# Rounding, loads and first splits around the end of a chunked-attention and two-layer feed-forward kernel's second up projection

## The chip, the cores and the metric

The kernel runs on one core of a Trainium2 chip. The metric is the device time of one execution, in microseconds (us). Engines are named as in the profile: PE is the matmul engine (TensorE) and PEld its weight load, DVE is VectorE, ACT is ScalarE, POOL is GpSimd, SP is SyncE, whose queue (SPq) issues every DMA of this kernel.

## What is computed

```python
attn_out = _attn_ref(**attn_kwargs)          # (4, 8, 768, 64), chunks of 32, softmax
x = attn_out.transpose(0, 2, 1, 3).reshape(B * S, H * D)   # 3072 x 512
h = x @ w_in;  r = maximum(h, 0);  g = s * (r * r) + b;  x = g @ w_out      # first layer
h = x @ w_in2; g = h - tanh(h);    return g @ w_out2                        # second layer
```

Both layers have 3072 tokens, a model width of 512 and a hidden width of 2048. All weights come as 64-bit floats and are read as pairs of 32-bit words.

## The kernel before, in words

Every fp32 product is made of three matmuls on rounded halves (`three`, lines 136 to 139): high by high, low by high, high by low. So each operand is first split: ACT rounds it to the high half, DVE subtracts to get the low half.

The program runs in stages: attention, the first layer's up projection (up 1), its down projection (down 1), then up 2 and down 2. The order on each engine is the order in which the code is written (`manual_schedule`, line 684); nothing reorders it. Each engine and the SP queue runs its own instructions in that order and waits where an operand or a buffer is not ready.

**Up 2** (lines 940 to 1000) goes over eight column blocks of the weights, `n` = 0 to 7. For each `n` there are three groups of 512-row token blocks. Groups 0 and 1 are plain products (`plain_column`, 12 matmuls each call, four calls per group; `plain_end` takes tanh on ACT at line 877 and subtracts on DVE at line 878). Group 2 (`quad`) computes its 2 by 2 blocks with seven products of Strassen's kind, P1 to P7 (`strassen`, six matmuls each). P1, P6, P5 and P3 add up in one PSUM bank, bank 0, and between them ACT copies the bank's state out (`copy`, line 900, into the tile `keep`): copy 1 after P1, copy 2 after P6, copy 3 after P5. P6 may not add to bank 0 before copy 1 has read it. P7 and P4 share bank 1, which `add` (line 903, DVE) reads before P4 adds to it. `curve` (lines 909, 910) makes the four tanh results, and `combine` (line 430) the sums that `end_out` stores to DRAM in the tiles `o2`, one per group, as `oa` (768 KB) and `ob` (1 MB).

Beside block `n`, the weights of block `n + 1` are made ready: ACT scales the raw words (line 144), DVE shifts, signs and fills them (lines 148, 152, 158), ACT rounds (`w2_high`, line 749), DVE subtracts (`w2_low`) and makes sums (`w2_sums`). In the last block (`n` = 7) the first weights of down 2 are prepared instead: quadrants 3 to 6 of `w_out` are fetched and converted (`load_quadrant`; "quadrant" here is one of its eight raw loads, 1 MB each, tile `raw`, line 364) and the weights of its first product are rounded (`high`, line 523, and `low`, line 528, tile `whl`).

**Down 2** (class `Down`, `run`, lines 564 to 580) walks over seven products (`ORDER`), three groups and two halves: 42 parts of 1 MB, read from `o2` (tile `part`, line 811). Each part is two entries. For entry `i`, `split` rounds 1024 columns on ACT (line 546) and subtracts on DVE (line 547) into a ring of three tiles, two entries ahead; `multiply(i)` does 12 matmuls. Part 0 holds the outputs of `n` = 0 to 3 of group 0; part 1 those of `n` = 4 to 7 of group 0; parts 2, 3 and 4, 5 the same of groups 1 and 2. The table `WEIGHTS` says behind which entry of a product the next product's weights are summed, rounded and subtracted; it serves down 1 and down 2. `between2` converts the last quadrants of `w_out` behind given entries.

In the text below, "multiply 7" is `multiply(7)` of down 2, "split 10" its `split(10)`; high and low half are the ACT and the DVE instruction of a split.

Of the kernel before, what the change touches and what calls it, by code (L numbers as in the profile page):

```python
# [48 lines left out]
"""  # L49

WEIGHTS = {
    (0, 1): [("sums", 1, 0)], (0, 2): [("high", 1, 0)], (0, 4): [("low", 1, 0)],
    (0, 5): [("sums", 1, 1)], (0, 6): [("high", 1, 1)], (0, 8): [("low", 1, 1)],
    (2, 0): [("sums", 3, 0)], (2, 1): [("high", 3, 0)], (2, 2): [("low", 3, 0)],
    (2, 4): [("sums", 3, 1)], (2, 5): [("high", 3, 1)], (2, 6): [("low", 3, 1)],
    (2, 8): [("sums", 4, 0)], (2, 9): [("sums", 4, 1)],
# [15 lines left out]
def tile_chunk_attention_two_ffn(  # L72
# [365 lines left out]
    class Down:  # L438


        def __init__(self, src, zmap, smap, whl, stream, ring, load, view, pick, bias, final, turn):
            self.src, self.zmap, self.smap, self.whl, self.stream, self.ring = src, zmap, smap, whl, stream, ring
            self.load, self.view, self.pick, self.bias, self.final = load, view, pick, bias, final
            self.z, self.zt, self.st, self.w, self.part, self.xs, self.ps = {}, {}, {}, {}, {}, {}, {}
            self.loaded, self.turn = 0, turn
            self.parts = [(p, g, h) for p in range(7) for g in range(NG) for h in range(2)]
            self.entries = [(p, g, h, e) for p, g, h in self.parts for e in range(2)]
            self.quads = list(zmap)
# [115 lines left out]
        def run(self, between):  # L564
            deep = len(self.stream)
            self.load_to(deep - 1)
            n = len(self.entries)
            for i in range(2):
                if i not in self.xs:
                    self.split(i)  # L570
            for i in range(n):
                if i + 2 < n:
                    self.split(i + 2)
                    if i % 2:
                        self.load_to(i // 2 + 1 + deep)
                self.multiply(i)
                p, k = divmod(i, 4 * NG)
                for step, q, half in WEIGHTS.get((p, k), ()):
                    getattr(self, step)(q, half)
                between(p, k)  # L580
# [117 lines left out]
    for j in range(2, NBLK):  # L698
        last = j == NBLK - 1
# [41 lines left out]
    def w2_signed(n):  # L741
        signed(w2_z[n], w2[n])

    def w2_filled(n):
        filled(w2_z[n], w2.pop(n))
# [120 lines left out]
    def plain_column(n, g, i, col):  # L866
        ps = bank2(2 + i)
        wh, wl = wi[2, n]
        for c in range(KD):
            xh, xl = x2_of(c, 1 - col, g)  # L870
            three(ps[:, col, 0:NB], wh[:, i, c, :], wl[:, i, c, :], xh, xl, c == 0, c == KD - 1)
# [11 lines left out]
    def strassen(name):  # L883
        acc = bank(chain[name])
        wh, wl = w2_hl[name]
        xh, xl = x2[operand[name], NG - 1]
        new_ = name in ("P1", "P7", "P2")
        for c in range(2):
            three(acc, wh[:, c], wl[:, c], xh[:, c], xl[:, c], c == 0 and new_, c == 1, not new_)

    def quad(n):
        g = NG - 1
        begin_out(n, g)
        oa = outs[n, g][0]
        keep = new(C_SNAP[0], 2 * NB, F32, "keep")
        snap = {1: keep[:, 0:NB], 2: keep[:, NB:2 * NB], 3: new(C_SNAP[1], NB, F32, "keep3")}
        rs = {}

        def copy(q):
            nc.scalar.activation(out=snap[q], in_=bank(0), func=AF.Copy)  # L900

        def add(o, q, k):
            nc.vector.tensor_tensor(out=oa[:, o], in0=snap[q], in1=bank(k), op=ALU.add)

        def curve(o, src):
            if o // 2 not in rs:
                rs[o // 2] = new(C_R[o // 2], 2 * NB, F32, "r2").rearrange("p (m t) -> p m t", m=2)
            r = rs[o // 2][:, o % 2]
            nc.scalar.activation(out=r, in_=src, func=AF.Tanh)
            nc.vector.tensor_tensor(out=oa[:, o], in0=src, in1=r, op=ALU.subtract)  # L910

        strassen("P1")
        copy(1)
        strassen("P7")
        strassen("P6")
        copy(2)
        yield
        strassen("P5")
        copy(3)
        strassen("P2")  # L920
        add(2, 3, 1)
        strassen("P3")
        add(1, 1, 2)
        strassen("P4")
        yield
        curve(0, bank(0))
        curve(1, oa[:, 1])
        curve(2, oa[:, 2])
        add(3, 2, 1)
        curve(3, oa[:, 3])  # L930
        yield
        end_out(n, g)
        yield
# [3 lines left out]
    def fetch(k, place=0):  # L937
        quads[k] = down2.load_quadrant(D_RAW[place])

    group = None  # L940
    for n in range(8):
        last = n == 7
        before = group
        begin_out(n, 0)
        for col in range(2):
            plain_column(n, 0, 0, col)
        if before is not None:
            next(before)
        if n in (2, 4, 6):
            quads[n // 2 - 1]()  # L950
        if not last:
            w2_load(n + 1)
        else:
            fetch(3, 0)
            fetch(4, 1)
        plain_end(n, 0, 0)
        if before is not None:
            next(before)
        if n == 0:
            t_split("T3")  # L960
            t_split("T2")
        w2_split(n)
        for col in range(2):
            plain_column(n, 0, 1, col)
        plain_end(n, 0, 1)
        end_out(n, 0)
        if n == 0:
            t_split("T1")
            t_split("T4")
        begin_out(n, 1)  # L970
        for col in range(2):
            plain_column(n, 1, 0, col)
        if last:
            quads[3]()
            down2.sums(0, 0)
            down2.high(0, 0)
            down2.low(0, 0)
            fetch(5, 0)
        else:
            w2_steps[0](n + 1)  # L980
        plain_end(n, 1, 0)
        if last:
            quads[4]()
            fetch(6, 1)
            down2.sums(0, 1)
            down2.high(0, 1)
            down2.low(0, 1)
            down2.load_to(0)
        else:
            for step in w2_steps[1:]:  # L990
                step(n + 1)
            if n in (1, 3, 5):
                fetch(n // 2)
        plain_column(n, 1, 1, 0)
        group = quad(n)
        next(group)
        plain_column(n, 1, 1, 1)
        plain_end(n, 1, 1)
        next(group)
        end_out(n, 1)  # L1000
    down2.load_to(1)
    down2.split(0)
    down2.split(1)
    next(group)

    def between2(p, k):
        if p == 0 and k == 0:
            next(group)
        if p == 0 and k == 3:
            quads[5]()  # L1010
            fetch(7, 0)
        if p == 1 and k == 6:
            quads[6]()
        if p == 1 and k == 9:
            quads[7]()
# [73 lines left out]
```

## Time and profile before

| | |
|---|---|
| median of three runs | 1091.02 us (1090.01 to 1091.71) |
| the profiled execution's own time | 1092.42 us |
| its span, first to last instruction | 1090.6 us |
| PE busy | 1055.8 us, 97% of the span |
| DVE busy | 813.3 us, 75% |
| ACT busy | 510.4 us, 47% |
| mean granted clock of PE | 0.993 |
| DMA | 242.15 MB, mean 222 GB/s |

Times in the trace are counted from the first instruction. Attention and up 1 end at 354 us, down 1 at 584, up 2 at 846; down 2 takes the rest, its last matmul starting at 1085.3. A matmul of 512 columns is shown with a duration near 0.39 us, but matmuls are pipelined: what one costs is the distance from its start to the next start. Idle time in square brackets stands before the instruction and names what ended it.

### The profile page before, as it was taken

How to read it: one execution, taken by the hardware profiler on the slowest of the kernel's cores; microseconds unless marked ns; L12 is line 12 of the kernel's file. 1: busy time of each engine (PE TensorE's matmuls, PEld its weight loads, DVE VectorE, ACT ScalarE, POOL GpSimd, SP SyncE). 2: the span in 40 equal slices, each digit the busy share in tenths (PEclk: the TensorE clock that was granted, in tenths of full speed). 3: DMA queues.
4: the chain of work that ended last, by engine and by line, in shares of the span. 5: the costliest groups of instructions: out<-in, count | busy, mean ns of one | idle time of the engine just before them, and what ended most of it. 6: DMA issues, size and time to landing. Idle time of an engine off the chain costs nothing.

```text
span 1090.6 us, 15131 instructions
## 1 busy us (share of the span) xinstructions
PE 1055.8 (97%) x6024; PEld 867.5 (80%) x6024; DVE 813.3 (75%) x969; ACT 510.4 (47%) x914; POOL 2.7 (0%) x24
## 2 busy tenths in 40 slices
PE   5999999999999999999999999999999799999998
PEld 4878888888888888888888777787778578888886
DVE  7997667777768866777787677787788778776654
ACT  7673655555433554455544333333334545444432
POOL 1000000000000000000000000000000000000000
PEclk8999999999999999999999999999999999999999
DMA  9864778775459756555541455655468975566751
GB/s 316 262 248 179 247 254 301 250 252 205 174 217 328 285 193 193 193 193 193 193 154 61 151 218 199 266 207 221 174 227 329 364 286 192 194 223 240 245 199 58
DMA packets 71686, 242.15 MB, mean 222 GB/s; under 512 B 5312, under 2 KB 5312, under 8 KB 61376
## 3 DMA queue, kind: packets, MB, share of 16 engines
q1 hardware_dynamic: 71616, 241.19, 61.8%
q8 instruction: 47, 0.77, 0.3%
q14 instruction: 23, 0.19, 0.1%
HBM read 146.80 MB, written 94.37 MB: 221 GB/s over the span
## 4 chain that ended last, share of the span: by engine, by line
PE 80%; DVE 9%; ACT 4%; DMA 4%; issue 2%; SPq 0%; ACTq 0%; DVEq 0%
PE pb L137 26%; PE pb L139 25%; PE pb L138 25%; PE pb L314 2%; PE pb L292 1%; DVE z L158 1%; PE pb L252 1%; DVE ob L430 1%; DVE z L152 1%; ACT sm L276 1%; DMA raw<-in_wo_dram 1%; DMA o<-oa 1%; DMA part<-o 1%; ACT w L749 1%; ACT r L877 1%
## 5 line engine op out<-in xcount | busy, mean ns | idle before, releaser
L137 PE MATMUL pb<-ringhringl,whl 128*128 128x512 f32 x672 | 262.4, 390 | 4.9 <-ACT ringhringl L546 4.9
L139 PE MATMUL pb<-ringhringl,whl 128*128 128x512 f32 x672 | 263.0, 391 | 3.0 <-DVE ringhringl L547 2.8
L138 PE MATMUL pb<-ringhringl,whl 128*128 128x512 f32 x672 | 262.0, 390 | 0.0
L547 DVE TENSOR_TENSOR ringhringl<-part,ringhringl 128x1024 fp32r<-128x1024 f32 x120 | 146.4, 1223 | 78.5 <-ACT ringhringl L546 78.5
L546 ACT ACTIVATE ringhringl<-part 128x1024 fp32r<-128x1024 f32 x120 | 126.3, 1059 | 150.2 <-PE pb L139 133.2
L137 PE MATMUL pb<-xh,w 128*128 128x512 f32 (+1 forms) x392 | 153.6, 392 | 0.6 <-DVE oa L415 0.3
L139 PEld LDWEIGHTS pb<-ringhringl,whl 128*128 128x128 f32 x672 | 126.4, 188 | 33.4 <-DVE ringhringl L547 6.6
L139 PE MATMUL pb<-xl,w 128*128 128x512 f32 (+1 forms) x392 | 151.2, 386 | 0.8 <-DVE xl L336 0.8
L138 PE MATMUL pb<-xh,w 128*128 128x512 f32 (+1 forms) x392 | 151.1, 386 | 0.5 <-DVE w L385 0.5
L137 PEld LDWEIGHTS pb<-ringhringl,whl 128*128 128x128 f32 x672 | 126.4, 188 | 31.5 <-ACT ringhringl L546 5.7
L138 PEld LDWEIGHTS pb<-ringhringl,whl 128*128 128x128 f32 x672 | 126.5, 188 | 26.4
L405 ACT ACTIVATE r<-pb 128x512 f32<-128x512 f32 x96 | 55.7, 591 | 100.7 <-PE pb L139 88.5
L415 DVE SCALAR_TENSOR_TENSOR oa<-pb,s_c,r 128x512 f32<-128x512 f32 x96 | 70.0, 745 | 29.2 <-ACT r L405 29.2
L137 PEld LDWEIGHTS pb<-xh,w 128*128 128x128 f32 x392 | 73.6, 188 | 17.7 <-DVE oa L415 1.8
L276 ACT ACTIVATE sm<-sm,nmx 128x96 f32<-128x96 f32 x192 | 69.1, 363 | 37.8 <-DVE nmx L270 37.8
L139 PEld LDWEIGHTS pb<-xl,w 128*128 128x128 f32 x392 | 73.6, 188 | 15.9 <-DVE xl L336 1.0
L138 PEld LDWEIGHTS pb<-xh,w 128*128 128x128 f32 x392 | 73.7, 188 | 14.9 <-DVE w L385 0.9
L542 DVE SCALAR_TENSOR_TENSOR ringhringl<-part,b_c,ringhringl 128x1024 fp32r<-128x1024 f32 x48 | 61.3, 1283 | 25.2 <-ACT ringhringl L541 24.8
L139 PE MATMUL pb<-x2hx2l,w 128*128 128x512 f32 x192 | 74.7, 389 | 0.0
L138 PE MATMUL pb<-x2hx2l,w 128*128 128x512 f32 x192 | 74.7, 389 | 0.0
L137 PE MATMUL pb<-x2hx2l,w 128*128 128x512 f32 x192 | 74.7, 389 | 0.0
L541 ACT ACTIVATE ringhringl<-part,b_c 128x1024 fp32r<-128x1024 f32 x48 | 54.9, 1147 | 36.3 <-PE pb L139 33.5
(131 smaller groups left out, 1394.8 us busy)
## 6 DMA issues: line engine op xcount, KB each, us to landing
o<-ob SPq DMA_DIRECT2D x48, 1024.0 KB, 4.9
part<-o SPq DMA_DIRECT2D x84, 512.0 KB, 4.6
part<-o SPq DMA_DIRECT2D x42, 1024.0 KB, 5.0
o<-oa SPq DMA_DIRECT2D x48, 768.0 KB, 3.9
raw<-in_wi_dram SPq DMA_DIRECT2D x16, 1024.0 KB, 7.2
raw<-in_wo_dram SPq DMA_DIRECT2D x16, 1024.0 KB, 7.2
qk<-in_qk_dram SPq DMA_DIRECT2D x24, 640.0 KB, 7.9
v<-in_vw_dram SPq DMA_DIRECT2D x24, 384.0 KB, 8.1
```

The lines of the kernel that those rows point to most:

```text
L137: nc.tensor.matmul(acc, lhsT=whi, rhs=xhi, start=first, stop=False, skip_group_check=more)
L138: nc.tensor.matmul(acc, lhsT=wlo, rhs=xhi, start=False, stop=False, skip_group_check=more)
L139: nc.tensor.matmul(acc, lhsT=whi, rhs=xlo, start=False, stop=last, skip_group_check=more)
L152: nc.vector.scalar_tensor_tensor(out=zi, in0=hi32, scalar=-(1 << 31), in1=zi, op0=ALU.bitwise_and, op1=ALU.bitwise_or)
L276: nc.scalar.activation(out=sm[:, h, :], in_=sm[:, h, :], func=AF.Exp, bias=nmx[:, h:h + 1], scale=1.0, accum_out=sums[:, h:h + 1],)
L314: nc.tensor.matmul(value_bank(u)[64 * g:64 * g + 64, c0:c0 + QE], lhsT=tv[0:KE, e, 2 * r + g, :], rhs=pt[0:KE, 4 * g + r, QE * e:QE * (e + ...
L405: nc.scalar.activation(out=r, in_=up_ps[j, t], func=AF.Relu)
L415: nc.vector.scalar_tensor_tensor(out=oab[j, q][0][:, 2 * i:2 * i + 2, k, :], in0=ps2, scalar=s_c[:, 0:1], in1=r2, op0=ALU.mult, op1=ALU.mult,)
L541: nc.scalar.activation(out=xh, in_=src, func=AF.Identity, bias=self.bias)
L542: nc.vector.scalar_tensor_tensor(out=xl, in0=src, scalar=self.bias, in1=xh.bitcast(F32), op0=ALU.add, op1=ALU.subtract)
L546: nc.scalar.activation(out=xh, in_=src, func=AF.Copy)
L547: nc.vector.tensor_tensor(out=xl, in0=src, in1=xh.bitcast(F32), op=ALU.subtract)
```

## The change

Four places of the written order change; no instruction is added or removed.

1. `WEIGHTS`, product 0: the two sums, the rounding and the low half of the next product's weights move from behind entries 1, 2, 4 (first half) and 5, 6, 8 (second half) to behind entries 4, 5, 6 and 8, 9, 10. Down 1 and down 2 both read the table.
2. `Down` gets `ahead`, 1 for down 1 (as before) and -1 for down 2: down 2's loads of parts are written two parts later.
3. In up 2, `quad` stops once more, behind copy 1. For `n` below 7, `w2_high`, `w2_low` and `w2_sums` are written there, between copy 1 and P7, and no longer ahead of P1.
4. In the last block, part 0 of down 2 is loaded in front of the two `w_out` loads; the rounding of the first product's weights moves behind quadrant 4's conversion; splits 0 and 1 are written behind copy 2; parts 1 and 2 are loaded ahead of group 1's stores; group 2's curves move behind multiply 0 and its stores behind multiply 1; quadrant 5's conversion and the fetch of quadrant 7 move from behind multiply 3 to behind multiply 7.

```diff
 WEIGHTS = {
-    (0, 1): [("sums", 1, 0)], (0, 2): [("high", 1, 0)], (0, 4): [("low", 1, 0)],
-    (0, 5): [("sums", 1, 1)], (0, 6): [("high", 1, 1)], (0, 8): [("low", 1, 1)],
+    (0, 4): [("sums", 1, 0)], (0, 5): [("high", 1, 0)], (0, 6): [("low", 1, 0)],
+    (0, 8): [("sums", 1, 1)], (0, 9): [("high", 1, 1)], (0, 10): [("low", 1, 1)],
...
-            self.loaded, self.turn = 0, turn
+            self.loaded, self.turn, self.ahead = 0, turn, 1 - 2 * turn
...
                     if i % 2:
-                        self.load_to(i // 2 + 1 + deep)
+                        self.load_to(i // 2 + deep + self.ahead)
...
         strassen("P1")
         copy(1)
+        yield
         strassen("P7")
...
         if last:
+            down2.load_to(0)
             quads[3]()
-            down2.sums(0, 0)
-            down2.high(0, 0)
-            down2.low(0, 0)
             fetch(5, 0)
...
         if last:
             quads[4]()
             fetch(6, 1)
-            down2.sums(0, 1)
-            down2.high(0, 1)
-            down2.low(0, 1)
-            down2.load_to(0)
+            for half in range(2):
+                down2.sums(0, half)
+                down2.high(0, half)
+                down2.low(0, half)
         else:
-            for step in w2_steps[1:]:
-                step(n + 1)
-            if n in (1, 3, 5):
-                fetch(n // 2)
+            w2_signed(n + 1)
+            w2_filled(n + 1)
         plain_column(n, 1, 1, 0)
         group = quad(n)
         next(group)
+        if not last:
+            w2_high(n + 1)
+            w2_low(n + 1)
+            w2_sums(n + 1)
+            if n in (1, 3, 5):
+                fetch(n // 2)
+        next(group)
+        if last:
+            down2.split(0)
+            down2.split(1)
         plain_column(n, 1, 1, 1)
         plain_end(n, 1, 1)
         next(group)
+        if last:
+            down2.load_to(2)
         end_out(n, 1)
-    down2.load_to(1)
-    down2.split(0)
-    down2.split(1)
-    next(group)

     def between2(p, k):
-        if p == 0 and k == 0:
+        if p == 0 and k in (0, 1):
             next(group)
-        if p == 0 and k == 3:
+        if p == 0 and k == 7:
             quads[5]()
             fetch(7, 0)
```

How the instructions stand in the built programs, first on ACT in up 2, block `n` = 0 (blocks 1 to 6 read the same). `w<-z` is the rounding of the next block's weights, `keep<-pb` are copies 1 and 2, `r<-pb` the tanh of a plain group; - is before, + is the change:

```order
 L877 ACTIVATE r_5172<-pb 128x1024
-L749 ACTIVATE w<-z 128x1024
-L900 ACTIVATE keep<-pb 128x512 x2
+L900 ACTIVATE keep<-pb 128x512
+L749 ACTIVATE w<-z 128x1024
+L900 ACTIVATE keep<-pb 128x512
 L877 ACTIVATE r_5232<-pb 128x1024
```

The rounding has moved from ahead of copy 1 to between copy 1 and copy 2.

Second, the SP queue in the last block of up 2. `o_0_79`, `o_1_80` and `o_2_81` are the tiles `o2` of groups 0, 1 and 2; rows with `part<-` are down 2's loads, rows with `<-oa` and `<-ob` are stores of up 2:

```order
 L864 DMA o_0_79<-ob 128x2048
+L811 DMA part<-o_0_79 128x4x512
 L364 DMA raw<-in_wo_dram 128x2048 x2
 L811 DMA part<-o_0_79 128x4x512
-L863 DMA o_1_80<-oa 128x1536
-L864 DMA o_1_80<-ob 128x2048
-L811 DMA part<-o_0_79 128x4x512
-L811 DMA part<-o_1_80 128x4x512 x2
+L811 DMA part<-o_1_80 128x4x512
+L863 DMA o_1_80<-oa 128x1536
+L864 DMA o_1_80<-ob 128x2048
+L811 DMA part<-o_1_80 128x4x512
```

Part 0 stands ahead of the two raw loads, and parts 1 and 2 stand behind them and ahead of group 1's stores.

Third, the passage from up 2 to down 2. On ACT before, from copies 1 and 2 of block 7 on (`r` from `oa` and the second `r` from `pb` are the curves of group 2, `ringhringl<-part` the high halves of splits):

```order
L900 ACTIVATE keep<-pb 128x512 x2
L877 ACTIVATE r_6735<-pb 128x1024
L900 ACTIVATE keep_6702<-pb 128x512
L546 ACTIVATE ringhringl<-part 128x1024 x2
L909 ACTIVATE r_6779<-pb 128x512
L909 ACTIVATE r_6779<-oa 128x512
L909 ACTIVATE r_6784<-oa 128x512 x2
```

and in the changed program:

```order
L900 ACTIVATE keep<-pb 128x512 x2
L546 ACTIVATE ringhringl<-part 128x1024 x2
L877 ACTIVATE r_6741<-pb 128x1024
L900 ACTIVATE keep_6702<-pb 128x512
L546 ACTIVATE ringhringl<-part 128x1024
L909 ACTIVATE r_6800<-pb 128x512
L909 ACTIVATE r_6800<-oa 128x512
L909 ACTIVATE r_6805<-oa 128x512 x2
```

The high halves of splits 0 and 1 stand behind copy 2, ahead of the last plain tanh and copy 3; that of split 2 stands ahead of the curves. On DVE in down 2's first product, before, from the sums of the next weights' first half (`s<-zq`) on; `zq` rows are quadrant 5's conversion, `whl` the low half of weights, `ringhringl` the low halves of splits:

```order
L501 TENSOR_TENSOR s_6836<-zq 128x1024
L501 TENSOR_TENSOR s_6838<-s_6836,zq 128x1024
L547 TENSOR_TENSOR ringhringl<-part,ringhringl 128x1024 x2
L148 TENSOR_SCALAR zq<-zq 128x1024
L152 SCALAR_TENSOR_TENSOR zq<-raw,zq 128x1024
L158 SCALAR_TENSOR_TENSOR zq<-raw,zq 128x1024
L547 TENSOR_TENSOR ringhringl<-part,ringhringl 128x1024
L528 TENSOR_TENSOR whl<-s_6838,whl 128x1024
```

and in the changed program:

```order
L501 TENSOR_TENSOR s_6881<-zq 128x1024
L501 TENSOR_TENSOR s_6883<-s_6881,zq 128x1024
L547 TENSOR_TENSOR ringhringl<-part,ringhringl 128x1024 x2
L528 TENSOR_TENSOR whl<-s_6883,whl 128x1024
L547 TENSOR_TENSOR ringhringl<-part,ringhringl 128x1024
L148 TENSOR_SCALAR zq<-zq 128x1024
L152 SCALAR_TENSOR_TENSOR zq<-raw,zq 128x1024
L158 SCALAR_TENSOR_TENSOR zq<-raw,zq 128x1024
L547 TENSOR_TENSOR ringhringl<-part,ringhringl 128x1024
L501 TENSOR_TENSOR s_6961<-zq 128x1024
L501 TENSOR_TENSOR s_6963<-s_6961,zq 128x1024
L547 TENSOR_TENSOR ringhringl<-part,ringhringl 128x1024 x2
```

Before, the sums stood between splits 3 and 4 and the conversion between splits 5 and 6; now the sums stand between splits 6 and 7, the conversion between splits 9 and 10, and the second half's sums between splits 10 and 11.

## Rows read from the trace of the kernel before

**Rows 1.** The page, part 1: busy time, share of the span, instructions of each engine.

```profile
PE 1055.8 (97%) x6024; PEld 867.5 (80%) x6024; DVE 813.3 (75%) x969; ACT 510.4 (47%) x914; POOL 2.7 (0%) x24
```

**Rows 2.** PE's waits: us in total, times, longest us.

```profile
PE pb L137 <- ACT keep L900: 7.8, 7, 2.0
...
PE pb L137 <- ACT ringhringl L546: 4.9, 2, 2.7
...
PE pb L139 <- DVE ringhringl L547: 2.8, 5, 1.5
```

**Rows 3.** Timeline of PE in up 2: start us, duration us, instruction [idle before].

```profile
608.25 0.51 PE L137 MATMUL pb<-t,shl 128*128 128x512 f32 x1 [2.00 <-ACT keep L900]
...
611.97 0.43 PE L137 MATMUL pb<-x2h,w 128*128 128x512 f32 x1
...
641.06 0.39 PE L139 MATMUL pb<-t,shl 128*128 128x512 f32 x1
642.35 0.50 PE L137 MATMUL pb<-t,shl 128*128 128x512 f32 x1 [0.91 <-ACT keep L900]
```

**Rows 4.** Timeline of DVE in block 1 of up 2.

```profile
639.50 1.23 DVE L158 SCALAR_TENSOR_TENSOR z<-raw,z 128x1024 int32<-128x1024 int32 x1
```

**Rows 5.** Timeline of ACT in block 1 of up 2.

```profile
640.76 1.06 ACT L749 ACTIVATE w<-z 128x1024 fp32r<-128x1024 f32 x1 [3.68 <-DVE z L158]
641.72 0.58 ACT L900 ACTIVATE keep<-pb 128x512 f32<-128x512 f32 x1
```

**Rows 6.** Stretches: us, busy by engine (instructions), granted PE clock, DMA share, GB/s.

```profile
608.25:611.90 3.65, 3.65 (x9) 2.93 (x10) 2.41 (x5) 0.60 (x1) 0.00 (x0) 0.55 0.00 0
...
857.70:861.10 3.40, 3.25 (x7) 2.14 (x8) 3.37 (x5) 1.88 (x2) 0.00 (x0) 0.51 1.05 385
```

**Rows 7.** Timeline of PE from block 7 of up 2 into down 2.

```profile
831.10 0.39 PE L137 MATMUL pb<-x2hx2l,w 128*128 128x512 f32 x1
...
844.70 0.39 PE L137 MATMUL pb<-t,w 128*128 128x512 f32 x1
...
845.83 0.39 PE L139 MATMUL pb<-t,w 128*128 128x512 f32 x1
...
879.10 0.50 PE L139 MATMUL pb<-ringhringl,whl 128*128 128x512 f32 x1
879.43 0.39 PE L137 MATMUL pb<-ringhringl,whl 128*128 128x512 f32 x1
```

**Rows 8.** Timeline of the SP queue around the end of up 2.

```profile
830.70 0.32 SPq L864 DMA_DIRECT2D o<-ob  x1
...
839.64 0.43 SPq L811 DMA_DIRECT2D part<-o  x1
...
847.29 5.63 SPq L811 DMA_DIRECT2D part<-o  x4
```

**Rows 9.** DMA issues, us to landing: at 830.7, 839.6 and 849.2 us, and after 900.

```profile
o<-ob SPq DMA_DIRECT2D x1, 1024.0 KB, 5.0
...
part<-o SPq DMA_DIRECT2D x1, 1024.0 KB, 7.6
...
part<-o SPq DMA_DIRECT2D x1, 1024.0 KB, 12.8
...
part<-o SPq DMA_DIRECT2D x29, 1024.0 KB, 4.9
```

**Rows 10.** Timeline of ACT: copy 2 of block 7, and the first sum of down 2.

```profile
838.10 0.60 ACT L900 ACTIVATE keep<-pb 128x512 f32<-128x512 f32 x1 [2.12 <-PE pb L139]
...
866.84 1.01 ACT L829 ACTIVATE sumX<-pb 128x1024 f32<-128x1024 f32 x1
```

**Rows 11.** Timeline of DVE: block 7's last weights, split 6, the second half's sums.

```profile
839.10 1.22 DVE L528 TENSOR_TENSOR whl<-zq,whl 128x1024 fp32r<-128x1024 f32 x1
...
872.02 1.22 DVE L547 TENSOR_TENSOR ringhringl<-part,ringhringl 128x1024 fp32r<-128x1024 f32 x1
...
875.43 1.22 DVE L501 TENSOR_TENSOR s<-zq 128x1024 f32<-128x1024 f32 x1
```

## The prediction

> **What bounds the kernel now.** I read the page's busy times first. PE is busy for 97% of the span [rows 1] and no other engine comes near, so whatever ends earlier must end PE's waits or make its matmuls start closer together. The second view is the list of PE's waits [rows 2]. Leaving out the first 30 us, which the change doesn't touch, three lines hold nearly all of it: seven waits for copy 1 (7.8 us, "ACT keep"), two for the high half of a split (4.9) and five for a low half (2.8). The third view is PE's timeline around them. It gives what an undisturbed matmul costs: 65 steps lie between 831.10 and 845.83 [rows 7], so 0.2266 us each. Against that, a wait costs more than its idle time. In block 1 of up 2 the step into P6 is 641.06 to 642.35 [rows 3], 1.29 us, that is 1.06 over an undisturbed one where the row says 0.91 idle: the idle time plus about 0.16. The step behind a wait is long too: 879.10 to 879.43 [rows 7], 0.33, which is 0.10 over. So a wait costs its idle time plus 0.27.
>
> **Up 2 (part 3 of the change).** Why does P6 wait? In block 1 filling the next weights starts on DVE at 639.50 and lasts to 640.73 [rows 4]; the rounding on ACT waits for that, starts at 640.76, and copy 1 follows at 641.72 [rows 5]. P1 itself had been done long before: its last matmul starts six steps ahead of the one at 641.06 [rows 3], at 639.70, and with the 0.39 that the rows show it ends at 640.09. So copy 1 is held by its neighbour in the queue, not by its data. In the new order it takes 640.1 to 640.7, P6 can start at 641.29 on its undisturbed step, and the rounding still starts at 640.76, since that is when its own data come. The wait is gone with 0.6 us to spare. What is late next would be copy 2: it stands behind the rounding now, which ends at 641.8, before P6 has ended (about 642.8); and P5, which needs copy 2, is 12 matmuls (2.7 us) further on. I cost that at nothing.
>
> The sum for seven blocks: 7.8 us idle [rows 2] plus 7 times 0.27 is 9.7. In block 0 a second cost hangs on the wait. From 608.25 to 611.97 nine steps take 3.72 us [rows 3] instead of 2.04, because the granted clock stands at 0.55 there [rows 6], close to the lower of its two levels (1.2 of 2.4 GHz). The dip follows straight on a wait of 2.00 us [rows 3], the longest of the seven [rows 2]. With the wait gone I take the dip as gone: 1.68, of which 0.10 is counted already. **Up 2 gains 11.3 us.**
>
> **The passage into down 2 (parts 2 and 4).** What is lost there today can be had in one line. The matmul at 879.10 is the third of multiply 8, number 98 counted from multiply 0's first. Undisturbed that first one stands one step behind 845.83, at 846.06, and number 98 at 868.27. It starts at 879.10 [rows 7], and one more 0.10 follows: 10.9 us, dip at 857.70 included [rows 6]. Behind it PE runs on without stops to its last matmul, so this loss reaches the end undiminished.
>
> The reason stands in the SP queue [rows 8]: part 0 is issued at 839.64, behind a raw load, and parts 1 to 4 only from 847.29, behind group 1's stores, which wait for DVE. Part 0 lands 7.6 us after its issue, at 847.2 [rows 9], when PE has stood since 846.2. In the new order part 0 follows the store of 830.70, so it is issued at 831.1. That store lands after 5.0 us, at 835.7. One megabyte behind another at 385 GB/s [rows 6] takes 2.7 us, so part 0 lands at 838.4, or at worst some way behind. Copy 2 of block 7 ends at 838.70 [rows 10], and split 0 is next on ACT: it just fits. Splits 0 and 1 then keep ACT for 1.9 us, until the last plain tanh can begin. On DVE the last low half of weights ends near 840.3 [rows 11]; two low halves, the plain subtraction (each of them 1.14 behind the one before) and the add that frees bank 1 bring it to 844.3, while P4 wants the bank at 844.70 [rows 7]: it fits by 0.4. Multiply 0 starts on its undisturbed step.
>
> Three losses stay.
> - **Parts 1 and 2.** Part 1 is issued behind the second raw load, which waits for quadrant 4's conversion: about 838.5, with part 0 and two raw loads, 8 us of transfer, in front. It should land near 846.5, then split 2, the four curves, split 3 and group 2's four sums queue on ACT and DVE in front of split 4. Bounds: nothing, where they all fit; 2.7, today's longest single wait [rows 2], which is this same part's, issued 8.8 later [rows 8]. I take 1.2, nearer to nothing, because most of the lateness goes.
> - **Quadrant 5's conversion** now stands in front of split 10's low half. Today the same chain, from the sum at 866.84 [rows 10] to the end of split 6 at 873.24 [rows 11], takes 6.4 us. In the new place the sum starts 0.43 behind multiply 7's last start, and multiply 10's third matmul, the first to need that low half, comes 27 steps (6.12) behind it. 0.43 + 6.4 + 0.08 to pass it on, less 6.12, is 0.8, and 0.1 for the step behind it: 0.9.
> - **The second half's sums** follow at once. Two of 1.2 each [rows 11] and a low half make 3.5; multiply 11's third matmul comes 2.8 later than multiply 10's. 0.7, with the step 0.8.
>
> Together 2.9 of the 10.9 stay; **the passage gains 8.0 us.** A price from a page: the Trainium skill, DMA: Bandwidth & Descriptors, section Anatomy of one DMA, fits the time of a DMA (of another issuing path) as 2.0 us plus its bytes at 436 GB/s. My estimate from it is 4.4 us for 1 MB; by it part 1 lands at 842.9, the first of the three losses vanishes and the time comes out 1.2 lower than below. The rows agree for a lone part (4.9) and not for parts in company (7.6 and 12.8) [rows 9].
>
> **What I cost at nothing.** `WEIGHTS` in down 1: PE's list has no wait for the biased splits of its first product [rows 2], so there is nothing to gain; the sums bring two 1.2 us instructions between splits there as here, but no conversion stands beside them. Bound: 1.5, as the third loss for both halves. Loads two parts later: a part's issue waits for its buffer, so the written place decides only whether a store stands in front. Counting the entries between a store's end and the split that needs the part, six entries or 16.3 us less 1.3 for the store's own instruction are left, 15.0, against 4.9 to land [rows 9]. Raw loads 2.7 later: their conversions stand behind multiply 7 and later, over 20 us on.
>
> **The sum.** 11.3 + 8.0 = 19.3. The profiled execution took 1092.42, so 1073.1 of that kind; it lies 1.4 above the median of the runs, 1091.02, so the median should come to **1071.7 us**.
>
> **Rivals.**
> - **Part 0 lands late and ACT and DVE hand it on.** Split 0 stands in front of the last tanh and copy 3 on ACT, and in front of the add that frees bank 1 on DVE. From 0.4 us of lateness on, P3 and P4 stop for the rest. For it: its margin is the smallest of all, and loads in company were slow [rows 9]. Against it: two transfers at most are in front. Half of the worst, 2.6 late, costs 2.2 and 0.4 for two steps, and about 0.7 more on split 4: 1075.0. At today's worst landing, 12.8, it is 5.2 late, P4 stops for over 2 us and a dip like those of rows 6 follows, 1.7: some 4.8 + 0.4 + 1.7 less the 1.2 of part 1, which then waits anyway: 1077.4. The Trainium skill, same page, section Queues, rings and completion order, says that each DMA engine takes descriptors in ring order; by that the raw load issued later can't push part 0 back, the sum stands and this rival has less for it, and the rows, where landings follow the issues, agree.
> - **Parts land early.** If part 1 takes 4.9 us like a lone one [rows 9], it is there at 843.4 and the first loss vanishes: 1070.5. Against it: 7.6 in company today [rows 9]. The page's fit, above, speaks for it.
> - **The wait moves on to copy 2.** If the rounding were as late as P6's end, P5 would stop in each block. It would give half of up 2's gain back: 1077.3. Against it: 2.7 us and more of cover in block 1.
> - **Slower: the loads of down 2 come too late.** With stores ahead of them on SP, each of the 24 parts of the last four products has 15.0 us from issue to use. If they land later than that, PE waits in each of them. The change loses only past 16 us to landing, where 24 times 0.9 is 21.6: 1093.3. Against it: 4.9 after 900 us, 12.8 at worst in the crowd [rows 9].
> - **The reordering in up 2 does nothing**: P6 is held by something other than copy 1. Then only the passage counts: 1083.0. The rows name copy 1 in all seven, so this is thin.
>
> **How the numbers follow.** The forecast 0.74, with its own range 1070 to 1074; late part 0 0.15; early parts 0.04; copy 2 0.03; up 2 unmoved 0.02; late loads of down 2 0.02, half of that so little late that it just uses up the gain. The lower end takes all three losses as nothing but 0.6: 1069.5. The upper end reaches into the first two rivals: 1077.0. A difference of 0.2% (2.2 us) is about what a measurement of this kernel can tell from none: faster 0.98, same 0.01, slower 0.01.
>
> **What would show it.** Right: "ACT keep" is gone from PE's waits and the clock stays full near 608; P6 follows P7 by 0.23 us; part 0 is issued near 831 and multiply 0 starts one step behind P4; waits of about 0.7 at multiplies 10 and 11. Wrong: PE waiting for L900 at P5, or for L903 at P4; a dip behind 846; waits for "part" after 900.

## The result and the profile after

The changed kernel takes 1072.95 us (median of 4 runs, 1072.36 to 1074.0) against 1090.95 in the same comparison: a ratio of 0.9837, with a 95% interval of 0.9819 to 0.9854. That is 18.0 us less, where 19.3 were forecast; 1071.7 was the forecast, 1069.5 to 1077.0 its range. The profiled execution took 1072.36 us with a span of 1070.6. One execution of experiment 2, a slow one of 2139.27 us, is left out of its median below.

The page, part 1, and the first three lines of the list of PE's waits (us in total, times, longest) of the changed kernel, beside [rows 1, 2]:

```profile
PE 1050.6 (98%) x6024; PEld 867.5 (81%) x6024; DVE 812.9 (76%) x969; ACT 511.5 (48%) x914; POOL 2.7 (0%) x24
```

```profile
PE pb L252 <- DMA qk<-in_qk_dram: 5.6, 3, 4.7
PE pb L292 <- DVE sm L286: 3.0, 3, 2.6
PE pb L139 <- DVE ringhringl L547: 2.1, 4, 0.7
```

The waits for copy 1 ("ACT keep") and for high halves ("ACT ringhringl") are gone from the list. What leads it now belongs to attention's start. Low halves still cost 2.1 us idle, 0.3 of it in down 1 as before.

Up 2, block 1, in the changed kernel. First ACT, where copy 1 now stands ahead of the rounding, then DVE, which ends the filling of the rounding's data:

```profile
635.84 0.60 ACT L900 ACTIVATE keep<-pb 128x512 f32<-128x512 f32 x1 [3.05 <-PE pb L139]
636.47 1.06 ACT L749 ACTIVATE w<-z 128x1024 fp32r<-128x1024 f32 x1
638.56 0.60 ACT L900 ACTIVATE keep<-pb 128x512 f32<-128x512 f32 x1 [1.03 <-PE pb L139]
```

```profile
635.21 1.22 DVE L158 SCALAR_TENSOR_TENSOR z<-raw,z 128x1024 int32<-128x1024 int32 x1
```

Copy 1 waits for P1 alone now and is done 0.03 us before the rounding starts, which starts 0.04 after its data at 636.43, as it did before [rows 4, 5]. Copy 2 waits for P6, with ACT idle for 1.03 before it. That cover is not the same in every block: ACT is idle for 0.39 in block 6, and in block 0 copy 2 follows the rounding with no idle time between. PE is not held in either. PE takes the step from P7 into P6 without a stop, 636.77 to 637.00:

```profile
636.77 0.39 PE L139 MATMUL pb<-t,shl 128*128 128x512 f32 x1
637.00 0.39 PE L137 MATMUL pb<-t,shl 128*128 128x512 f32 x1
```

The passage, in the changed kernel: the SP queue, then the landing time of the part issued at 819.25, then ACT, then PE from P4 into multiply 0 and at its three stops in down 2.

```profile
818.84 0.32 SPq L864 DMA_DIRECT2D o<-ob  x1
819.25 0.39 SPq L811 DMA_DIRECT2D part<-o  x1
822.01 4.58 SPq L364 DMA_DIRECT2D raw<-in_wo_dram  x2
826.68 0.94 SPq L811 DMA_DIRECT2D part<-o  x2
```

```profile
part<-o SPq DMA_DIRECT2D x1, 1024.0 KB, 8.1
```

```profile
826.24 0.60 ACT L900 ACTIVATE keep<-pb 128x512 f32<-128x512 f32 x1 [2.12 <-PE pb L139]
827.33 2.01 ACT L546 ACTIVATE ringhringl<-part 128x1024 fp32r<-128x1024 f32 x2 [0.49 <-DMA part<-o]
```

```profile
833.97 0.39 PE L139 MATMUL pb<-t,w 128*128 128x512 f32 x1
834.20 0.39 PE L137 MATMUL pb<-ringhringl,whl 128*128 128x512 f32 x1
...
846.38 0.50 PE L139 MATMUL pb<-ringhringl,whl 128*128 128x512 f32 x1 [0.66 <-DVE ringhringl L547]
...
863.61 0.50 PE L139 MATMUL pb<-ringhringl,whl 128*128 128x512 f32 x1 [0.61 <-DVE ringhringl L547]
...
867.14 0.50 PE L139 MATMUL pb<-ringhringl,whl 128*128 128x512 f32 x1 [0.52 <-DVE ringhringl L547]
```

Part 0 lands 8.1 us after its issue, at 827.3, and split 0 starts 0.49 later than ACT could have begun it. That is inside the margin, by little: the add that frees bank 1 ends 0.3 us before P4 starts. Multiply 0 starts one step behind P4, where there were 2.55 us before, from 845.83 [rows 7] to this row of the kernel before:

```profile
848.38 0.50 PE L137 MATMUL pb<-ringhringl,whl 128*128 128x512 f32 x1 [2.16 <-ACT ringhringl L546]
```

The three stops left are at multiplies 4, 10 and 11. With the step of 0.34 behind each they cost 0.93, 0.89 and 0.79 (a step into the third matmul of 1.04, 1.00 and 0.90, each less 0.2266, and 0.11): 2.6 of the 10.9 us.

Where the 20.0 us between the two spans came from, by the starts of PE's matmuls: up 2, from its first matmul to its last, takes 250.0 us instead of 261.5 (11.5 gained), from there to the last matmul of all 231.2 instead of 239.4 (8.2), and down 1 began 0.4 earlier, at 353.76 instead of 354.14.

### The profile page after: what moved, and what is told of

The parts are those of the page before. It is cut to its first block, busy times and chain, and to the rows that moved or that the text cites. A ratio compares the mean times of both kernels' runs of the same rounds, so it can differ in the third digit from the quotient of the medians.

```text
span 1070.6 us, 15128 instructions
## 1 busy us (share of the span) xinstructions
PE 1050.6 (98%) x6024; PEld 867.5 (81%) x6024; DVE 812.9 (76%) x969; ACT 511.5 (48%) x914; POOL 2.7 (0%) x24
## 4 chain that ended last, share of the span: by engine, by line
PE 87%; DVE 7%; ACT 2%; DMA 2%; issue 1%; SPq 0%; ACTq 0%; DVEq 0%
PE pb L137 28%; PE pb L139 27%; PE pb L138 27%; PE pb L314 2%; PE pb L292 2%; PE pb L252 1%; ACT sm L276 1%; DVE ob L430 1%; DMA part<-o 1%; DVE ringhringl L547 1%; DVE oa L415 1%; DMA raw<-in_wi_dram 1%; DVE z L158 1%; DVE w L385 1%; DVE z L152 0%
## 5 line engine op out<-in xcount | busy, mean ns | idle before, releaser
L137 PE MATMUL pb<-ringhringl,whl 128*128 128x512 f32 x672 | 261.5, 389 | 0.0
L138 PE MATMUL pb<-ringhringl,whl 128*128 128x512 f32 x672 | 261.5, 389 | 0.0
L137 PEld LDWEIGHTS pb<-xh,w 128*128 128x128 f32 x392 | 73.6, 188 | 17.6 <-DVE oa L415 1.6
```

The costliest lines, as they stand in the source:

```text
L137: nc.tensor.matmul(acc, lhsT=whi, rhs=xhi, start=first, stop=False, skip_group_check=more)
L138: nc.tensor.matmul(acc, lhsT=wlo, rhs=xhi, start=False, stop=False, skip_group_check=more)
```

## The experiments

Every time below is a median of its own comparison, beside the kernel before on the same chip; ratios are to that kernel, with their 95% interval.

**1. Up 2 alone.** The kernel before, with part 3 of the change and nothing else.

```diff
         copy(1)
+        yield
...
-            for step in w2_steps[1:]:
-                step(n + 1)
+            w2_signed(n + 1)
+            w2_filled(n + 1)
...
+        next(group)
+        if not last:
+            w2_high(n + 1)
+            w2_low(n + 1)
+            w2_sums(n + 1)
...
```

> The kernel before with part 3 of the change alone: the next weights' rounding between copy 1 and P7 in blocks 0 to 6 of up 2. Theory (copy 1 was held only by the rounding ahead of it on ACT): all seven waits for copy 1 go, with the half-clock stretch behind the first, 11.3 us; the passage into down 2 keeps its loss of 10.9. Time 1090.95 - 11.3 = 1079.7 us. Rival (the wait moves on to copy 2, which now stands behind the rounding, and P5 stops instead): half comes back, 1085. Rival (the two gains overlap, the passage gets worse when up 2 gets shorter): above 1081, with a loss at the passage of more than 10.9.

1080.16 us against 1090.95, 0.9899 (0.9884 to 0.9915): 10.8 us gained. "ACT keep" is gone from PE's list, so the wait did not move on to copy 2. Up 2 takes 250.0 us in the trace, as in the changed kernel. The passage keeps stops of the old kind. From up 2's last matmul to the end this execution takes 238.7 us, where the two profiles of the kernel before have 239.4 and 239.6, so a little of its gain, up to 1 us, was not up 2's:

```profile
PE pb L139 <- DVE ringhringl L547: 4.0, 6, 1.5
...
PE pb L137 <- ACT ringhringl L546: 2.5, 2, 2.1
```

**2. The passage alone.** The changed kernel with part 3 undone.

```diff
-            w2_signed(n + 1)
-            w2_filled(n + 1)
+            for step in w2_steps[1:]:
+                step(n + 1)
...
-        if not last:
-            w2_high(n + 1)
-            w2_low(n + 1)
-            w2_sums(n + 1)
...
```

> The changed kernel with part 3 undone: up 2 rounds ahead of P1 again, all else as changed. Theory (the gains lie in different stretches and add up): the seven waits for copy 1 are back, 7.8 us idle and 11.3 us in all, the half-clock stretch near 608 included; the passage loses only 2.6. Time 1072.95 + 11.3 = 1084.3 us by the changed kernel, 1090.95 - 8.3 = 1082.7 by the kernel before. Rival (the parts depend on each other): the sum of the gains of this run and of part 3 alone differs from 18.0 us by more than 2.

1083.73 us (median of five), 0.9936 (0.992 to 0.9951): 7.2 us gained. The two gains add to 18.0, which is what the whole change gained (17.3 when it was measured a second time, see experiment 6), so they lie side by side and neither needs the other. The trace says the same: from up 2's last matmul to the end this run takes 231.2 us, as the changed kernel does. The seven waits are back, the first of them of 2.00 us again. But here the clock does not fall behind it, as the stretches view shows (us, busy by engine, granted clock; the place answers to 608.25 in [rows 6]):

```profile
PE pb L137 <- ACT keep L900: 7.9, 7, 2.0
```

```profile
608.49:612.20 3.71, 3.71 (x16) 3.08 (x17) 2.43 (x5) 0.60 (x1) 0.00 (x0) 1.00 0.00 0
```

**3. Part 0 behind the two raw loads.**

```diff
         if last:
-            down2.load_to(0)
             quads[3]()
...
             fetch(6, 1)
+            down2.load_to(0)
```

> The changed kernel with part 0's load behind the two w_out loads, splits 0 and 1 still behind copy 2. Theory (part 0's place on the SP queue carries the passage, and its margin is half a microsecond): part 0 is issued near 826.7 instead of 819.3 and lands near 835 instead of 827.3; split 0 stands in front of the last tanh and copy 3, so P3 and P4 stop for about 6 us, a half-clock stretch of 1.7 follows, the wait at multiply 4 goes (0.9): 1073 + 6.5 + 1.7 - 0.9 = 1080 us. Rival (the landing is hidden anyway, since multiply 0 comes 7 us behind copy 2): 1073, no wait of PE before multiply 0.

1079.65 us, 0.9894 (0.9879 to 0.991), against 1072.95 for the changed kernel: 6.7 us of the gain lost by one load's place. In this run's timelines of ACT and PE:

```profile
826.27 0.60 ACT L900 ACTIVATE keep<-pb 128x512 f32<-128x512 f32 x1 [2.12 <-PE pb L139]
833.86 2.00 ACT L546 ACTIVATE ringhringl<-part 128x1024 fp32r<-128x1024 f32 x2 [6.99 <-DMA part<-o]
835.77 1.00 ACT L877 ACTIVATE r<-pb 128x1024 f32<-128x1024 f32 x1
836.67 0.59 ACT L900 ACTIVATE keep<-pb 128x512 f32<-128x512 f32 x1
```

```profile
837.31 0.80 PE L137 MATMUL pb<-x2hx2l,shl 128*128 128x512 f32 x1 [5.64 <-ACT keep L900]
```

ACT stands 6.99 us for the part; the tanh and copy 3 queue behind the split, and P3 waits 5.64 for copy 3. The clock is at half behind it (0.51 from 837.31 to 841.20), and the wait at multiply 4 is gone. This was the first rival of the prediction, made to happen: the mechanism is real, and the changed kernel escapes it by a few tenths of a microsecond.

**4. The loads' old distance.** From entry 3 on; the first loads stay, because part 5 may not be read before group 2's stores.

```diff
-                        self.load_to(i // 2 + deep + self.ahead)
+                        self.load_to(i // 2 + deep + (self.ahead if i < 3 else 1))
```

> The changed kernel with down 2's loads written at their old distance again from entry 3 on (the loads up to part 4 stay where the change has them). Theory (a load waits for its buffer, the written place decides only about stores in front of it): within 0.2% of the changed kernel, 1073 us, PE's waits in down 2 the same four. Rival (the earlier place matters, in either direction: loads in front of stores delay the stores or come sooner): over 2 us from 1073, with PE waiting for part or for the output tile after 900 us.

1072.68 us, 0.9833 (0.9817 to 0.9848), and PE's list shows the same 2.1 us, 4 times, for low halves. From entry 3 on, part 2 of the change is worth nothing in time by itself.

**5. The old table for down 1 alone.**

```diff
+OLD = {(0, 1): [("sums", 1, 0)], ...}
...
-                for step, q, half in WEIGHTS.get((p, k), ()):
+                for step, q, half in (OLD if p == 0 and not self.turn else WEIGHTS).get((p, k), ()):
```

> The changed kernel with the table's old places for down 1 alone. Theory (PE has no wait in down 1's first product with either order): 1073 us, no wait of PE between 354 and 440 us in either, the same waits after it. Rival (the later sums or rounding gain or cost in down 1): a difference of more than 1 us in the length of down 1.

1072.63 us, 0.9833 (0.982 to 0.9847). The matmuls show no stop in down 1's first product in either order, and the four stops of 0.2 to 0.5 in the later ones are there in both. Down 1 takes 230.2 us in both: it doesn't notice.

**6. The old table, for down 1 and down 2, and the old place of quadrant 5's conversion.** Experiments 6, 7 and 8 stand in one comparison with the changed kernel measured a second time, which came to 1072.56 us, 0.9837 (0.9824 to 0.9851), with stops of 0.65, 0.62 and 0.51 at the same three multiplies.

```diff
-        if p == 0 and k == 7:
+        if p == 0 and k == 3:
             quads[5]()
```

(and `WEIGHTS`, product 0, as before)

> The changed kernel with part 1 undone: the table as before, and quadrant 5's conversion behind multiply 3 again, which the second half's sums need. Theory (down 1 doesn't notice; in down 2 the sums fall on top of group 2's four sums and push split 4's low half 2.4 us further back, while the losses at multiplies 10 and 11 go): a wait of about 3 us at multiply 4, maybe a half-clock stretch behind it, 0.3 at multiply 8: 1073 + 2.4 + 0.3 - 1.7 = 1074, or 1075.7 with such a stretch. Rival (the table is what brings the passage its gain): several us worse, 1078. Rival (the table costs more than it saves): under 1072.

> The changed kernel once more, as the measure for the three others of this group. Both theories: 1073 us, three losses at multiplies 4, 10 and 11 of down 2 (0.9, 0.9 and 0.8 us), none in up 2.

1074.74 us, 0.9855 (0.9842 to 0.9869). One long stop at multiply 4 takes the place of three, 3.07 of the 3.4 us idle:

```profile
PE pb L139 <- DVE ringhringl L547: 3.4, 2, 3.1
```

In the trace that is 3.5 us with its steps, against 2.6: 0.9 worse; the medians say 2.2 worse, with intervals that overlap. In the two profiled executions 1.2 of the 2.2 lie ahead of everything that the edit touches: down 1 begins at 354.8 here and at 353.6 in the changed kernel. The trace is what shows the new place in down 2: it is worth about 1 us, and it keeps the sums off the stretch in which group 2's four sums are also due. The half-clock stretch that the expectation allowed for did not come: behind the wait of 3.07 us, longer than any that the kernel before has in down 2, the clock stays full (stretches view):

```profile
849.78:853.40 3.62, 3.62 (x16) 2.97 (x17) 3.55 (x4) 2.19 (x3) 0.00 (x0) 1.00 1.02 427
```

**7. The scaling of quadrant 5 one multiply earlier.**

```diff
-        if p == 0 and k == 7:
-            quads[5]()
+        if p == 0 and k == 6:
+            quads[5].begin()
+        if p == 0 and k == 7:
+            quads[5].end()
             fetch(7, 0)
```

> The changed kernel with the scaling of quadrant 5 (ACT) behind multiply 6 instead of behind multiply 7 and the sum that follows it; the rest of its conversion stays. Theory (the losses at multiplies 10 and 11 are one chain: DVE stands idle for 2.4 us until that scaling, then the conversion and two sums are late by less than that): both losses go, 1.7 us, 1071.3. Rival (DVE has too much work there, and the idle time would only be filled by later work): the losses stay, 1073, or move to the weights' rounding behind multiply 9.

1070.86 us, 0.9819 (0.9805 to 0.9832), 1.7 under the changed kernel in the same comparison. The two intervals still overlap a little, but each of the four runs (1070.02 to 1071.27) is shorter than each of the changed kernel's five (1072.07 to 1073.86). The stops at multiplies 10 and 11 are gone from the trace. On DVE, the changed kernel first, then this run:

```profile
859.21 0.70 DVE L148 TENSOR_SCALAR zq<-zq 128x1024 int32<-128x1024 int32 x1 [2.41 <-ACT zq L144]
```

```profile
856.16 1.23 DVE L547 TENSOR_TENSOR ringhringl<-part,ringhringl 128x1024 fp32r<-128x1024 f32 x1
857.30 0.69 DVE L148 TENSOR_SCALAR zq<-zq 128x1024 int32<-128x1024 int32 x1
```

The 2.41 us for which DVE stood idle in front of the conversion were spent waiting for a scaling that stood on ACT behind the sum of multiply 7. One instruction moved by one multiply removes the wait and with it both losses.

**8. And group 2's four sums behind multiply 2.**

On top of experiment 7:

```diff
-        if p == 0 and k in (0, 1):
+        if p == 0 and k in (0, 2):
             next(group)
```

> As the run before, and group 2's four sums and stores behind multiply 2 instead of multiply 1. Theory (the loss at multiply 4 is its low half standing behind those four sums of 0.6 us): the loss at multiply 4 goes too, 0.9 us, and PE has no wait left in down 2: 1070.4, 2.6 under the changed kernel. Rival (part 1 or 2 lands too late for multiply 4 whatever stands in front): the loss stays, 1071.3. Rival (part 5, which waits for the store that is made later, comes too late): a new wait for part at multiply 10.

1070.76 us, 0.9821 (0.9807 to 0.9834): nothing more gained that the medians show. The stop at multiply 4 is gone, as the theory said, and one of the same size stands at multiply 11, which the last rival had named with its cause (there for multiply 10). This run's PE, then its ACT:

```profile
866.95 0.50 PE L139 MATMUL pb<-ringhringl,whl 128*128 128x512 f32 x1 [0.53 <-DVE ringhringl L547]
```

```profile
861.04 1.06 ACT L546 ACTIVATE ringhringl<-part 128x1024 fp32r<-128x1024 f32 x1 [2.29 <-DMA part<-o]
```

ACT waits 2.29 us for part 5.

**9. Group 2's first store ahead of part 4's load.**

On top of experiment 8:

```diff
-            self.load_to(deep - 1)
+            self.load_to(deep - 1 - self.turn)
...
         curve(3, oa[:, 3])
+        if n == 7:
+            nc.sync.dma_start(out=o2[g][:, n, 0:3], in_=oa[:, 1:4])
...
```

> As the run with both (scaling of quadrant 5 early, group 2's four sums behind multiply 2), and group 2's first store (oa) on the SP queue ahead of part 4's load, which waits for another store to land. There the loss had moved to multiply 11: part 5, which waits for oa to land, was issued at 853.9, 10 us after its words were ready, and landed at 861.0, so ACT stood 2.3 us for it. Theory (what is late next is that store's place on the queue): part 5 is issued near 848.5 and lands before 858, the wait of 0.5 us at multiply 11 goes, PE has no wait in down 2's first product: 1070.0, 0.8 under the run with both. Rival (multiply 11 is held by DVE's work, conversion and two sums, whenever part 5 lands): the wait stays, 1070.8. Rival (part 4 is pushed back too far): a new wait at multiply 8.

1072.8 us against 1091.76, 0.9825 (0.9811 to 0.9838): my theory fell. The stop of 0.51 at multiply 11 is still there, and two of 0.19 and 0.24 have come at multiplies 3 and 10. In this run's ACT timeline split 6 now waits for part 3 and split 10 still waits for part 5:

```profile
849.52 2.01 ACT L546 ACTIVATE ringhringl<-part 128x1024 fp32r<-128x1024 f32 x2 [1.43 <-DMA part<-o]
...
860.03 2.01 ACT L546 ACTIVATE ringhringl<-part 128x1024 fp32r<-128x1024 f32 x2 [0.86 <-DMA part<-o]
```

The store moved by 1.9 us only (843.1 against 844.9) and took 9.0 us to land. Part 5 landed 1.0 earlier than in experiment 8, at 859.95, and part 3 landed 2.0 later, at 849.44. At multiply 11 it is no longer part 5 that comes last. Split 10's high half ends at 861.1, and its low half starts at 862.85, directly behind quadrant 5's conversion:

```profile
859.72 0.69 DVE L148 TENSOR_SCALAR zq<-zq 128x1024 int32<-128x1024 int32 x1
860.44 1.23 DVE L152 SCALAR_TENSOR_TENSOR zq<-raw,zq 128x1024 int32<-128x1024 int32 x1
861.70 1.23 DVE L158 SCALAR_TENSOR_TENSOR zq<-raw,zq 128x1024 int32<-128x1024 int32 x1
862.85 1.22 DVE L547 TENSOR_TENSOR ringhringl<-part,ringhringl 128x1024 fp32r<-128x1024 f32 x1
```

DVE has no idle time from 856.3 to the end of split 11's low half at 867.6, and its conversion starts 1.7 later than in experiment 8, behind split 6's low half, which part 3 made late. So the first rival, DVE's work, names what holds multiply 11 in this run. From 835 to 871 us the DMA engines are 97% busy in the run of experiment 8, at 355 GB/s, and the order that brought one transfer forward pushed others back. Whether fewer bytes in this stretch would free the last 0.8 us was not tried.

**10. The kernel before, profiled a second time.**

> The kernel before once more, for a second profile of it. In the changed kernel with part 3 undone the wait of 2.00 us for copy 1 in block 0 was there again, and no half-clock stretch behind it. Theory (a wait near 2 us sometimes brings such a stretch and sometimes not, so the 3.6 us that two of them cost in the first profile are no fixed part of the time): the waits are the same to 0.1 us, the stretches lie elsewhere or are fewer, and the span differs by their cost, 1.6 to 1.9 us each. Rival (a stretch belongs to its wait): half clock at 608 to 612 and at 857.6 to 861 again, span 1090.6.

1090.22 us against 1091.09, 0.9996 (0.9986 to 1.0006): no difference, as it should be. Its span is 1088.2, 2.4 below the first profile's. The wait of 2.00 us in block 0 is there again, and the clock stays full behind it; in the passage a longer stretch than before stands behind another, shorter wait:

```profile
607.62:611.30 3.68, 3.68 (x16) 3.07 (x17) 2.42 (x5) 0.60 (x1) 0.00 (x0) 1.00 0.00 0
846.96:852.60 5.64, 5.64 (x13) 4.45 (x14) 4.17 (x6) 1.79 (x4) 0.00 (x0) 0.50 0.95 300
```

So a half-clock stretch is no property of the wait in front of it. It came behind some waits of 2 us and more and not behind others, and in the changed kernel, whose longest wait from down 1 on is 0.7, none was seen from there on in either of its two profiles.

Two parts of the theory fell. The waits are not the same to 0.1 us: copy 1's in block 6 is 0.91 where it was 1.24, and the wait of 2.70 at multiply 2 is gone. And a stretch does not always cost 1.6 to 1.9 us. In up 2 it cost 1.7; in the passage the second profile has a longer one and is hardly slower for it (239.6 us against 239.4 to the last matmul), because multiply 2 waits for split 2, and split 2 for its part, in both: it starts 12.0 us behind up 2's last matmul here and 11.8 in the first profile.

## Why the prediction was right, and where it was off

**Up 2.** Each step came as written: copy 1 was held by its neighbour in ACT's queue, the rounding starts when its data come, copy 2 is covered. Alone it gave 10.8 us (experiment 1) where 11.3 were forecast. The cover of copy 2 had been worked out for block 1 alone; in block 0 none was left, and copy 2 came just in time there, 2.72 us behind copy 1 as in block 1.

**The passage.** Part 0 was forecast to be issued one queue step behind the store, and was; to land 7.3 us later, and took 8.1; split 0 was to fit, and came 0.49 late inside P4's margin, which at 0.3 to 0.4 us was small enough that some luck was in it. The three losses that were to stay are the three that stayed: forecast 1.2, 0.9 and 0.8, measured 0.93, 0.89 and 0.79. The last two were worked out as chains of instructions and came out as such. The 1.2 was a choice between bounds of 0 and 2.7, and that it lies 0.3 off is partly luck. Its chain is as written, though: part 1 landed at 835.0, where 846.5 less up 2's 11.3 had been forecast, and moving group 2's four sums out of the way ends the stop (experiment 8). 8.0 us were forecast, the trace shows 8.2 and the medians of the run with the passage alone 7.2.

**The costs of nothing.** The table in down 1, the loads two parts later and the later raw loads cost nothing that these runs resolve (experiments 4 and 5; the later raw loads were not tested alone, and PE has no stop behind multiply 11).

**What was off** is the size of one term: "With the wait gone I take the dip as gone: 1.68". The lengths of the stages in the traces show it, in us by the starts of PE's matmuls (the last column runs from up 2's last matmul to the last of all; down 1 takes 230.2 in each):

| profile | down 1 begins | up 2 | passage and down 2 |
|---|---|---|---|
| before, first | 354.1 | 261.5 | 239.4 |
| before, second (experiment 10) | 353.5 | 259.5 | 239.6 |
| up 2 alone (experiment 1) | 354.0 | 250.0 | 238.7 |
| passage alone (experiment 2) | 354.4 | 260.0 | 231.2 |
| changed | 353.8 | 250.0 | 231.2 |

Against the profile that was read, up 2 gained 11.5. Against the second one it gained 9.5: there the dip in block 0 is missing (1.7) and the wait in block 6 is 0.3 shorter. The run that kept its waits has no dip in block 0 either (experiment 2). So the dip belongs to some executions and not to the kernel: without it the sum for up 2 is 9.7, and 9.7 and 8.0 are 17.7. The gain between medians is 18.0 in the first comparison and 17.3 in the second, and the spans of the changed kernel and of the second profile differ by 17.6.

The step from spans to medians missed as well. The prediction took 1.4 off because its profile was that much longer than the median run; the profiled run of the changed kernel lies 0.6 under its own median, so 20.1 between the profiled runs became 18.0 between the medians. How often the dip comes in runs without a profile is not shown. Their mean granted clocks alone don't tell: of the eleven runs of the kernel before beside experiments 1 to 4, the longest (1093.75) has the highest, 0.997.

**The rivals.** Late part 0 is the one that mattered: made to happen it cost 6.7 us (experiment 3). The wait did not move on to copy 2, up 2's reordering was not idle, the loads of down 2 never came late, and parts did not land as early as a lone one. The sentence on the Trainium skill's fit (DMA: Bandwidth & Descriptors, Anatomy of one DMA), by which the first loss would vanish, is answered by the rows: in this passage parts took 8.1 and 8.4 us where a lone one takes 4.9, so the first loss stayed, at 0.9.

## What to carry to other kernels

When a wait names a short instruction, look at what stands ahead of it in its engine's queue: copy 1 needed 0.6 us and had its data, and was held by a rounding that had not. Check each instruction that is moved across such a point for what it now stands in front of. The rounding cost nothing in its new place, and the same check found the one dangerous place beforehand (a split that waits for a DMA, in front of a copy that PE waits for). Take a profile's half-clock stretches out of a sum before setting it against a median, unless a second profile has them in the same places. And compare the lengths of the stages in two profiles, not only their spans: a gain of 1 us in down 2 is clear there, while the start of down 1 alone moves by 1.8 us from profile to profile.

## What the runs showed of the hardware

- The half-clock stretches: behind waits of 2.00, 2.10, 2.14, 2.70 and 5.64 us in four profiles, 3.3 to 5.6 us long, granted clock 0.50 to 0.55. The same wait of 2.00 us was followed by full clock in two other profiles, and so was a wait of 3.07 us (experiment 6). I had taken wait and stretch to belong together.
- The 1 MB loads of parts 0, 1 and 2 in the changed kernel, with others issued just ahead of them, took 8.1, 8.4 and 11.4 us from issue to landing; after 900 us in the kernel before the median is 4.9 [rows 9]. What part 5 gained by an earlier place, 1.0 us, part 3 lost twice over (experiment 9).
- How long the stages ahead of down 1 take varies: down 1 began between 353.5 and 355.3 us in the profiles of these kernels, and none of the edits touches what stands before it. It is most of what two spans differ by where PE's stops are the same (1070.3 to 1070.9 in the changed kernel's two profiles and those of experiments 4 and 5, with down 1 beginning at 353.6 to 354.1).
